# Value products over two 64-key halves side by side, summed by VectorE, in a talking-heads attention with a linear expert

## The chip, the cores and the metric

The kernel runs on one core of one Trainium2 chip. The time is the device time of one execution in microseconds (us). Three runs of the kernel before gave 1441.68, 1441.87 and 1443.87 us; the median, 1441.87 us, is what the change is measured against.

## The reference

Eight batches of 12 heads, 448 positions, 64 channels per head. The scores are mixed across heads before the softmax and the weights are mixed across heads after it; then come the value products, and the joined heads go through a bilinear layer and two linear ones:

```python
scores = scale * np.matmul(q, k.transpose(0, 1, 3, 2))
scores = np.einsum('bhij,hg->bgij', scores, w_pre)
attn = np.exp(scores - np.max(scores, axis=-1, keepdims=True))
attn = attn / (np.sum(attn, axis=-1, keepdims=True) + 1e-09)
attn = np.einsum('bhij,hg->bgij', attn, w_post)
attn_out = np.matmul(attn, v)
x = attn_out.transpose(0, 2, 1, 3).reshape(B * S, H * D)
out = ((x @ w1) * (x @ w2)) @ w3 @ w_out
```

The change touches only `attn_out = attn @ v`, for batches 2 to 7.

## The kernel before

**Steps.** The queries of a batch are cut into 45 tiles of 10 (the last has 8). One step `n` of the main loop in `run` belongs to one such tile; two tiles are worked on together, so even and odd steps differ. A step holds these pieces, and every engine executes its instructions in the order in which `run` writes them (nothing is reordered by a scheduler):

- the expert's matmuls, handed out by `advance` in a number per step that a table `shares` sets (tiles `eg` and `eo` for the first two batches, then `e`, `e1o`, `e2o`, `e3o` by pairs of batches; lines 522, 553, 702);
- in some odd steps, the value products `av` (line 301, PSUM tile `psa`);
- in odd steps, `post` (line 260, tile `pso`): the head mix after the softmax, 56 small matmul instructions that also turn the weights so that keys lie on partitions; then `mix` (line 220, tile `psm`): the head mix before the softmax; then `qk` (line 174, tile `psq`): scores of a coming batch, which go to HBM and are read back by head.

ScalarE copies `pso` into `mt` (line 274) and `psq` into `st` (lines 179 and 180), takes the exponentials (line 235), and VectorE takes the row extremes from `psm` (line 227).

**The value products.** `mt` holds the mixed weights of 150 queries (15 tiles; the last stretch of a batch has 148), with 128 keys on the partitions and four key blocks `j`. Keys are 448 = 3 x 128 + 64. In the fourth block each partition half holds the same 64 keys: `post` writes the last key block of row half `s` to partition half `s`, and zeros, set once before the loop, stand in the other half. So in block 3 the first 64 partitions hold only the queries 0 to 4 of each ten, and the last 64 partitions only the queries 5 to 9; `layouts` doubles the last 64 rows of `v` to match. `av(b, a, g)` handles one pair of heads `g` in stretch `a` (0, 1, 2) of batch `b`: for each key block and each of the two heads one fp32 matmul with 128 contraction rows and 64 output columns, which the profile shows as two MATMUL records. Three pairs share a PSUM bank and are emitted in one step; the next three come two steps later. So a batch has 6 such groups of 3 calls, 4 of them 150 queries wide and 2 of them 148 wide.

**PSUM banks.** `psa` and the first `psq` of a step's `qk` use bank 0; the second half of `qk` uses bank 1; `psm` uses 2 and 3, `pso` 4 and 5, the expert 6 and 7. For batches from the third on (`b >= ONE`, `ONE = 2`), ScalarE copies a finished `psa` bank to an SBUF tile `xd` (line 308), and the next step's start issues its store to `x_d` in HBM on the SyncE queue. In the first two batches ScalarE writes `xh` from the bank and VectorE then reads the bank again for `xl` (lines 322 and 323).

`ends` holds the closing work (PSUM reads) of groups with their bank numbers; `do_ends` emits it. `bank(i)` emits pending closing work first if bank `i` is among it.

Of the kernel before, what the change touches and what calls it, by code (L numbers as in the profile page):

```python
# [10 lines left out]
ALU = mybir.AluOpType  # L11
# [4 lines left out]
B, H, S, D = 8, 12, 448, 64  # L16
DM, FF = 768, 1024
HP = H // 2
IB = 10
GI = H * IB  # L20
NB = -(-S // IB)
QT, NJ = 128, 4
GB = 15
NG = NB // GB
KF, K1 = FF // 128, DM // 128
IH = IB // 2
HK = H * IH
PP = 64
# [9 lines left out]
ONE = 2  # L38
# [12 lines left out]
class Kernel:  # L51
# [237 lines left out]
    def cols(self, a):  # L289
        return slice(a * GB * IB, min((a + 1) * GB * IB, S))  # L290

    def av(self, b, a, g):
        nc, cols = self.nc, self.cols(a)
        W = cols.stop - cols.start
        if g % 3 == 0:
            self.psa = self.bank(0, f"psa{b}_{a}_{g}")[:, :3 * GB * IB].rearrange("p (g i) -> p g i", g=3)
        v, mt = self.vs[b, g], self.mt[b, a]
        for j in range(NJ):
            for s in range(2):
                rows = slice(s * D, (s + 1) * D)  # L300
                nc.tensor.matmul(self.psa[rows, g % 3, :W], v[:, j, rows], mt[:, j, 2 * g + s, :W],  # L301
                                 start=(j == 0), stop=(j == NJ - 1))
        if g % 3 == 2 and b >= ONE:
            q, dst = self.psa[:, :, :W], self.x_d[b][g // 3][:, :, cols]
            x = self.xq.tile([128, 3, GB * IB], F32, tag="x", name=f"xd{b}_{a}_{g}")[:, :, :W]

            def leave():
                nc.scalar.copy(x, q)
                self.later.append(store)

            def store():
                nc.sync.dma_start(dst, x)
                self.x_made[b] += 1

            self.ends.append((0, leave))
        elif g % 3 == 2:
            if b not in self.xs:
                pool = self.xp[b % 2]
                self.xs[b] = [pool.tile([128, K1, S], F32R, tag=f"x{t}", name=f"x{t}{b}") for t in "hl"]
            h, l = (x[:, g - 2:g + 1, cols] for x in self.xs[b])  # L320
            q = self.psa[:, :, :W]
            self.ends.append((0, lambda: nc.scalar.copy(h, q)))
            self.soon.append((0, lambda: nc.vector.tensor_tensor(l, q, h.bitcast(F32), op=ALU.subtract)))
        if a == NG - 1:
            self.later.append(self.load_v)
# [726 lines left out]
```

## Time and profile before

| what | value |
|---|---|
| median of 3 runs | 1441.87 us (1441.68 to 1443.87) |
| the profiled execution's own time | 1437.83 us |
| its span, first to last instruction | 1436.1 us |
| mean granted TensorE clock | 0.986 |
| MATMUL records of the value products | 2304, of them 1728 in batches 2 to 7 |
| groups of three calls in batches 2 to 7 | 36 (24 of 150 queries, 12 of 148) |
| their first and last start | 398.2 and 1262.5 us |
| ScalarE copies `xd` | 36, median 535 ns |

TensorE's busy time counts records whose ends are modelled; the starts of matmuls are what tells their pace. "PE" are matmuls, "PEld" weight loads, which overlap matmuls. In the timeline, a row gives start, length, engine, line, operation, tiles, shapes and how many records were merged; in the chain of waits a row gives start, length, and what was on the path that ended last.

### The profile page before, as it was taken

To read this page: it belongs to the slowest core of one execution; us is meant where nothing else is said; L and a number is where in the kernel's file an instruction comes from. 1 tells how busy PE (TensorE), PEld (TensorE's weight loads), DVE (VectorE), ACT (ScalarE), POOL (GpSimd) and SP (SyncE) were. 2 spreads that over 40 slices of the span, in tenths; PEclk is the share of its full clock that TensorE was granted. 3 is DMA by queue.
4 is the path that set the end of the run, shared out by engine and by line. 5 is a ranking of instruction groups with operands and counts; after the bars stand their busy time and mean duration, and the time that the engine had idled before them with its cause. 6 is when DMAs were issued, how large, how long until landed. Compare 5 with 4: busy or idle time off the path is not lost.

```text
span 1436.1 us, 45775 instructions
## 1 busy us (share of the span) xinstructions
PE 1382.4 (96%) x18684; PEld 1055.2 (73%) x18684; DVE 741.1 (52%) x1497; ACT 832.4 (58%) x1952; POOL 620.3 (43%) x754
## 2 busy tenths in 40 slices
PE   5889999999999999999999999999999999999998
PEld 2457786776677667776777777777777777899988
DVE  6867566767544544432444436334444446345563
ACT  4867666777766666665656556556555445422231
POOL 2433233434433544532345336334335446446693
PEclk7989999999999999999999999999999999999999
DMA  8998789999999999999989979799879757698775
GB/s 294 366 326 279 236 270 322 320 312 317 324 286 348 355 356 330 362 346 349 287 275 290 320 259 280 249 323 354 288 229 281 241 177 223 195 337 270 231 232 171
DMA packets 203761, 416.87 MB, mean 290 GB/s; under 512 B 20528, under 2 KB 120112, under 8 KB 203472
## 3 DMA queue, kind: packets, MB, share of 16 engines
q1 hardware_dynamic: 203552, 413.94, 87.6%
q8 instruction: 149, 2.44, 0.7%
q14 instruction: 60, 0.49, 0.1%
HBM read 279.77 MB, written 134.09 MB: 288 GB/s over the span
## 4 chain that ended last, share of the span: by engine, by line
PE 82%; DMA 8%; DVE 4%; ACT 2%; issue 1%; POOL 1%; SPq 0%; DVEq 0%; POOLq 0%; ACTq 0%
PE e L702 21%; PE psa L301 11%; PE pso L260 10%; PE psm L220 9%; PE psq L174 7%; PE eg L522 5%; PE psf L360 4%; PE eo L553 4%; PE e2o L702 4%; PE e1o L702 4%; PE e3o L702 4%; DMA wu<-w_d 3%; DMA r<-raw_d 2%; DMA raw_d<-st 2%; ACT e L235 1%
## 5 line engine op out<-in xcount | busy, mean ns | idle before, releaser
L247 POOL TENSOR_SCALAR w<-wpo,ri 128x60 f32<-128x60 f32 x360 | 180.7, 518 | 485.1 <-DVE ri L245 465.3
L227 DVE TENSOR_REDUCE mn<-psm 128x1 f32<-128x448 f32 x360 | 207.7, 618 | 321.6 <-PE psm L220 321.3
L274 ACT COPY mt<-pso 128x480 f32<-128x480 f32 x352 | 197.9, 621 | 185.8 <-PE pso L260 185.6
L702 PE MATMUL e<-eh,wu 128*128 128x448 f32 x1008 | 296.8, 371 | 6.4 <-DVE c L656 3.2
L235 ACT ACTIVATE e<-psm,mn 128x448 f32<-128x448 f32 x360 | 226.8, 643 | 7.9 <-DVE mn L227 7.9
L702 PEld LDWEIGHTS e<-eh,wu 128*128 128x128 f32 x1008 | 187.5, 188 | 52.2 <-issue 26.8
L260 PEld LDWEIGHTS pso<-w,e 60*64 60x64 f32 x10080 | 175.2, 135 | 51.0 <-issue 42.5
L220 PE MATMUL psm<-r,wsc 60*64 60x448 f32 (+1 forms) x1440 | 191.2, 550 | 19.1 <-DVE cx L124 8.3
L260 PE MATMUL pso<-w,e 60*64 60x60 f32 x10080 | 199.1, 224 | 0.4 <-ACT mt L274 0.3
L702 PE MATMUL e<-el,wu 128*128 128x448 f32 x504 | 186.9, 371 | 0.0
L301 PE MATMUL psa<-mt,v 128*64 128x150 f32 (+1 forms) x2304 | 156.9, 292 | 4.1 <-ACT st L179 4.1
L301 PEld LDWEIGHTS psa<-mt,v 128*64 128x64 f32 x2304 | 143.6, 137 | 20.1 <-ACT st L179 6.7
L174 PE MATMUL psq<-kq 64*64 64x448 f32 x1176 | 154.6, 542 | 2.4 <-ACT st L179 2.4
L656 DVE TENSOR_TENSOR c<-c,e 128x448 f32<-128x448 f32 x168 | 101.7, 618 | 87.7 <-PE e L702 82.9
L179 ACT COPY st<-psq 128x448 f32<-128x448 f32 x162 | 86.4, 533 | 73.7 <-ACT mt L274 34.1
L522 PE MATMUL eg<-xh,wu 128*128 128x448 f32 x384 | 119.2, 381 | 6.3 <-DMA wu<-w_d 6.3
L641 POOL TENSOR_TENSOR el<-x,eh 128x448 fp32r<-128x448 f32 x90 | 103.7, 1170 | 32.8 <-ACT eh L640 29.9
L702 PEld LDWEIGHTS e<-el,wu 128*128 128x128 f32 x504 | 94.6, 188 | 22.5 <-issue 14.1
L174 PEld LDWEIGHTS psq<-kq 64*64 64x64 f32 x1176 | 60.8, 135 | 56.4 <-issue 28.8
L522 PEld LDWEIGHTS eg<-xh,wu 128*128 128x128 f32 x384 | 71.9, 190 | 38.7 <-issue 24.0
L244 DVE TENSOR_SCALAR sa<-sm 128x2 f32<-128x2 f32 x180 | 34.9, 194 | 113.6 <-ACT e L235 113.1
L180 ACT COPY st<-psq 128x448 f32<-128x448 f32 x162 | 87.6, 541 | 0.0
(99 smaller groups left out, 2010.1 us busy)
## 6 DMA issues: line engine op xcount, KB each, us to landing
r<-raw_d SPq DMA_DIRECT2D x344, 210.0 KB, 5.1
raw_d<-st SPq DMA_DIRECT2D x138, 448.0 KB, 6.1
wu<-w_d SPq DMA_DIRECT2D x104, 384.0 KB, 6.7
wu<-s_d SPq DMA_DIRECT2D x96, 384.0 KB, 4.8
wu<-w_d SPq DMA_DIRECT2D x51, 512.0 KB, 5.5
kq<-kq SPq DMA_DIRECT2D x42, 448.0 KB, 7.0
wu<-s_d SPq DMA_DIRECT2D x36, 512.0 KB, 4.9
x<-x_d SPq DMA_DIRECT2D x72, 224.0 KB, 5.7
```

The source lines that it names most:

```text
L174: nc.tensor.matmul(ps[s][z * PP:(z + 1) * PP], t[rows, q:q + PP], t[rows, k:k + S], start=True, stop=True)
L220: nc.tensor.matmul(ps[s][c * PP:(c + 1) * PP, :S], self.wsc[k], r[k, c], start=True, stop=True)
L227: self.nc.vector.tensor_reduce(mn[:, s:s + 1], self.psm[m][s][:, :S], axis=AX.X, op=ALU.min)
L235: nc.scalar.activation(e, p[:, :S], AF.Exp, bias=mn[:, s:s + 1], scale=-1.0, accum_out=sm[:, s:s + 1])
L247: nc.gpsimd.tensor_scalar_mul(w2[:, s], self.wpo, ri[:, s:s + 1])
L260: nc.tensor.matmul(self.pso[c][z * PP:(z + 1) * PP, at:at + HK], e[k, j * PP:(j + 1) * PP], w2s[k, s], start=True, stop=True)
L274: self.nc.scalar.copy(dst.rearrange("p j g (s i) -> p j s g i", s=2), src)
L301: nc.tensor.matmul(self.psa[rows, g % 3, :W], v[:, j, rows], mt[:, j, 2 * g + s, :W], start=(j == 0), stop=(j == NJ - 1))
L522: nc.tensor.matmul(p, u[:, k % (K1 // 2), x], xs[y][:, k], start=(k == 0 and t == 0), stop=(k == K1 - 1 and t == 2))
L641: nc.gpsimd.tensor_tensor(lo, x, hi.bitcast(F32), op=ALU.subtract)
L656: nc.vector.tensor_tensor(a[out], a[to[0]], p, op=ALU.add)
L702: nc.tensor.matmul(p, w[:, k, x], ops[m, k][y], start=(k == 0 and t == 0), stop=(k == nk - 1 and t == 2))
```

## The change

For batches 2 to 7 `av` opens two banks, 0 and 1. Key blocks 0 to 2 are cut into partition halves: the products of keys on partitions 0 to 63 go to bank 0, those on 64 to 127 to bank 1. Block 3 is taken for each half with the columns in which that half is not zero: 5 queries of each ten, through a three-dimensional view (`halves`), and where the stretch is 148 wide a second piece of 5 or 3 columns for the incomplete tile. After ScalarE's copy of bank 0, VectorE adds bank 1 to it. Batches 0 and 1 keep their products.

```diff
+    def halves(self, w, z):
+
+        n = w // IB
+        yield lambda t: t[:, :n * IB].rearrange("p (u s i) -> p u s i", s=2, i=IH)[:, :, z]
+        if w % IB:
+            yield lambda t: t[:, n * IB + z * IH:min(n * IB + (z + 1) * IH, w)]
+
     def av(self, b, a, g):
...
         if g % 3 == 0:
-            self.psa = self.bank(0, f"psa{b}_{a}_{g}")[:, :3 * GB * IB].rearrange("p (g i) -> p g i", g=3)
+            self.psa = [self.bank(z, f"psa{b}_{a}_{g}_{z}")[:, :3 * GB * IB].rearrange("p (g i) -> p g i", g=3)
+                        for z in range(1 + (b >= ONE))]
         v, mt = self.vs[b, g], self.mt[b, a]
-        for j in range(NJ):
+        for j in range(NJ - (b >= ONE)):
             for s in range(2):
                 rows = slice(s * D, (s + 1) * D)
-                nc.tensor.matmul(self.psa[rows, g % 3, :W], v[:, j, rows], mt[:, j, 2 * g + s, :W],
-                                 start=(j == 0), stop=(j == NJ - 1))
+                for z, psa in enumerate(self.psa):
+                    keys = slice(z * PP, (z + 1) * PP) if b >= ONE else slice(0, 128)
+                    nc.tensor.matmul(psa[rows, g % 3, :W], v[keys, j, rows], mt[keys, j, 2 * g + s, :W],
+                                     start=(j == 0), stop=(j == NJ - 1), skip_group_check=b >= ONE)
+        if b >= ONE:
+            for s in range(2):
+                rows = slice(s * D, (s + 1) * D)
+                for z, psa in enumerate(self.psa):
+                    keys = slice(z * PP, (z + 1) * PP)
+                    for part in self.halves(W, z):
+                        nc.tensor.matmul(part(psa[rows, g % 3]), v[keys, NJ - 1, rows], part(mt[keys, NJ - 1, 2 * g + s]),
+                                         start=False, stop=True, skip_group_check=True)
         if g % 3 == 2 and b >= ONE:
-            q, dst = self.psa[:, :, :W], self.x_d[b][g // 3][:, :, cols]
+            (q, r), dst = (t[:, :, :W] for t in self.psa), self.x_d[b][g // 3][:, :, cols]
...
                 nc.scalar.copy(x, q)
+                nc.vector.tensor_tensor(x, x, r, op=ALU.add)
                 self.later.append(store)
...
-            self.ends.append((0, leave))
+            self.ends += [(0, leave), (1, lambda: None)]
```

On TensorE, the end of the first group of batch 2. Before (`eo` is the expert's matmul ahead, `psa_0_0` the group's bank, x8 are the eight matmuls of one head pair):

```order
L553 MATMUL eo_0_5896<-eh_4_4931,wu_5796 128x448
L301 MATMUL psa_0_0_5984<-mt_0_5258,v_0_5280 64x150 x8
L301 MATMUL psa_0_0_5984<-mt_0_5258,v_1_5282 64x150 x8
L301 MATMUL psa_0_0_5984<-mt_0_5258,v_2_5284 64x150 x8
L260 MATMUL pso_141<-w_5885,e_0_5864 64x60
L260 MATMUL pso_142<-w_5885,e_0_5864 64x60
```

Now, the last rows of the third pair (`psa_0_0_0` is in bank 0, `psa_0_0_1` in bank 1):

```order
L311 MATMUL psa_0_0_0_5984<-mt_0_5258,v_2_5284 64x150
L311 MATMUL psa_0_0_1_5985<-mt_0_5258,v_2_5284 64x150
L319 MATMUL psa_0_0_0_5984<-mt_0_5258,v_2_5284 64x15x5
L319 MATMUL psa_0_0_1_5985<-mt_0_5258,v_2_5284 64x15x5
L319 MATMUL psa_0_0_0_5984<-mt_0_5258,v_2_5284 64x15x5
L319 MATMUL psa_0_0_1_5985<-mt_0_5258,v_2_5284 64x15x5
L260 MATMUL pso_141<-w_5885,e_0_5864 64x60
L260 MATMUL pso_142<-w_5885,e_0_5864 64x60
```

A pair is 8 matmuls before and 16 now: 12 of full width and 4 of 75 columns. In a group of 148 queries it is 20; there the fourth block reads as follows, with two matmuls in a row on the same half:

```order
L311 MATMUL psa_2_0_1_7541<-mt_2_6774,v_0_5280 64x148
L319 MATMUL psa_2_0_0_7540<-mt_2_6774,v_0_5280 64x14x5
L319 MATMUL psa_2_0_0_7540<-mt_2_6774,v_0_5280 64x5
L319 MATMUL psa_2_0_1_7541<-mt_2_6774,v_0_5280 64x14x5
L319 MATMUL psa_2_0_1_7541<-mt_2_6774,v_0_5280 64x3
```

On VectorE at the same group, before (`sa`, `ri` belong to the softmax's sums, `y` to sums of expert weights, `mn` are the row extremes that wait for `psm`):

```order
L244 TENSOR_SCALAR sa_5976<-sm_5961 128x2
L245 RECIPROCAL ri_5977<-sa_5976 128x2
L463 TENSOR_TENSOR y_0_5954<-wu_5796 128x512
L227 TENSOR_REDUCE mn_6061<-psm_0_6039 128x1
L227 TENSOR_REDUCE mn_6061<-psm_1_6040 128x1
```

Now:

```order
L244 TENSOR_SCALAR sa_5976<-sm_5961 128x2
L245 RECIPROCAL ri_5977<-sa_5976 128x2
L482 TENSOR_TENSOR y_0_5954<-wu_5796 128x512
L327 TENSOR_TENSOR xd_0_2_6034<-xd_0_2_6034,psa_0_0_1_5985 128x450
L227 TENSOR_REDUCE mn_6087<-psm_0_6065 128x1
L227 TENSOR_REDUCE mn_6087<-psm_1_6066 128x1
```

The add stands between the softmax's small operations and the next row extremes, 36 times in all. ScalarE's and SyncE's rows keep their order, and no transfer is added. Of the 36 groups, 34 are followed by `pso` (the last two by `e`), and 28 of these by `psm` and then `psq`.

More of the change, by code (lines that the diff above doesn't have):

```diff
@@ L320, in av @@
             h, l = (x[:, g - 2:g + 1, cols] for x in self.xs[b])
-            q = self.psa[:, :, :W]
+            q = self.psa[0][:, :, :W]
             self.ends.append((0, lambda: nc.scalar.copy(h, q)))
```

## The prediction

> **What bounds the kernel now.** First the page's busy times and its chain of waits, by engine and by line:
>
> ```profile
> PE 1382.4 (96%) x18684; PEld 1055.2 (73%) x18684; DVE 741.1 (52%) x1497; ACT 832.4 (58%) x1952; POOL 620.3 (43%) x754
> PE 82%; DMA 8%; DVE 4%; ACT 2%; issue 1%; POOL 1%; SPq 0%; DVEq 0%; POOLq 0%; ACTq 0%
> PE e L702 21%; PE psa L301 11%; PE pso L260 10%; PE psm L220 9%; PE psq L174 7%; PE eg L522 5%; PE psf L360 4%; PE eo L553 4%; PE e2o L702 4%; PE e1o L702 4%; PE e3o L702 4%; DMA wu<-w_d 3%; DMA r<-raw_d 2%; DMA raw_d<-st 2%; ACT e L235 1%
> ```
>
> TensorE is the path, and the value products are 11% of it. Then the windows (columns: PE, PEld, DVE, ACT, POOL busy with counts, granted clock, DMA share, GB/s), since the changed groups run from 398 to 1262 us, and TensorE's waits between 380 and 700 us:
>
> ```profile
> 400.00:500.00 100.00, 97.68 (x1558) 72.55 (x1554) 47.29 (x96) 62.83 (x148) 41.06 (x46) 1.00 0.98 333
> 600.00:700.00 100.00, 97.55 (x1479) 72.79 (x1478) 31.63 (x77) 62.16 (x149) 29.52 (x45) 1.00 1.01 344
> 800.00:900.00 100.00, 99.68 (x1474) 75.97 (x1473) 48.00 (x101) 59.98 (x140) 47.31 (x58) 1.00 0.88 283
> PE eg L522 <- DMA wu<-w_d: 6.3, 5, 2.8
> ```
>
> Up to about 700 us the DMA engines are as full as TensorE; after that TensorE alone is. A third of the groups (12: the 8 wide and 4 narrow of batches 2 and 3) lies in the first stretch. There TensorE waited 6.3 us, five times, for expert weights.
>
> The chain in order of time around the first changed group, and a 148-wide one:
>
> ```profile
> 395.79 2.43 PE eo L553 x11
> 398.22 3.21 PE psa L301 x48
> 401.43 1.01 PE pso L260 x47
> 402.44 0.76 PE psm L220 x8
> ...
> 494.18 3.17 PE psa L301 x48
> ```
>
> So a group's 3.21 us (3.17 at 148) are on the path whole. How they are made up, the timeline of TensorE over short stretches shows:
>
> ```profile
> 398.15 0.35 PE L301 MATMUL psa<-mt,v 128*64 128x150 f32 x2
> 398.15 0.48 PE L301 MATMUL psa<-mt,v 128*64 128x150 f32 x4
> 400.75 0.68 PE L301 MATMUL psa<-mt,v 128*64 128x150 f32 x8
> 401.13 0.30 PE L301 MATMUL psa<-mt,v 128*64 128x150 f32 x2
> 401.36 0.28 PE L260 MATMUL pso<-w,e 60*64 60x60 f32 x4
> 401.36 0.34 PE L260 MATMUL pso<-w,e 60*64 60x60 f32 x8
> 401.36 0.57 PE L260 MATMUL pso<-w,e 60*64 60x60 f32 x24
> 402.22 0.54 PE L220 MATMUL psm<-r,wsc 60*64 60x448 f32 x1
> 402.23 0.22 PE L260 MATMUL pso<-w,e 60*64 60x60 f32 x1
> 402.98 0.98 PE L174 MATMUL psq<-kq 64*64 64x448 f32 x8
> ```
>
> Records start in rounds. Value products go two abreast (the two heads' 64 columns): the last 8 records take 0.68 us, the last 2 0.30, so three rounds are 0.38 and one is 0.127 us. A group is 24 rounds, 3.05 us. The 64 x 64 products go four abreast: `pso`'s records 9 to 24 add 0.57 - 0.34 = 0.23 us in four rounds, 0.058 each at 60 columns; `psm`'s 8 records, two rounds at 448 columns, take from 402.22 to 402.98, 0.38 each. And a change of shape costs: `psa`'s last round begins at 401.13, so the next could at 401.26, but `pso` starts at 401.36, 0.10 late; and `pso`'s second round begins 0.10 after the first (0.34 less a record's 0.22 and the stagger of 0.02) in place of 0.058. Together 0.145 us. Between `pso`, `psm` and `psq`, all 64 x 64, there is no such gap.
>
> **The change, part by part.**
>
> *Rounds of 64 x 64.* A half-key matmul has `pso`'s form and order (row half 0, row half 1, next column half), so I cost it four abreast. No row has 150 columns in that form; the straight line through 60 columns (0.058) and 448 (0.38) has 0.83 ns a column and gives 0.133 us at 150, 0.131 at 148, 0.0705 at 75 and 0.066 at 70. The other end is the two-abreast price, 0.127 and its half, 0.064. I take the line: its rows have the same shape.
>
> - 150 wide: 36 full logical matmuls are 18 rounds, 12 of 75 columns are 6. 18 x 0.133 + 6 x 0.0705 = 2.82 us against 3.05: 0.23 saved. At the other end 0.37.
> - 148 wide: before, 3.05 - (3.21 - 3.17) = 3.01. Now 18 x 0.131 + 6 x 0.066, and 6 rounds more of 5 or 3 columns. A round that short is between the line's 0.012 and the 0.058 of 60 columns; I take 0.058, because weights are loaded for it all the same. Sum 3.10: 0.09 lost (at the other end 0.18 saved).
>
> 24 x 0.23 - 12 x 0.09 = **4.4 us**.
>
> *Shape changes.* The expert ahead of the group is 128 x 128, so entering costs the same: the second round starts 0.48 - 0.30 = 0.18 after the first against 0.127 now, and would again. Leaving for `pso` is now without a change of shape: 34 groups x 0.145 = **4.9 us**. The two last groups go to the expert and gain nothing here.
>
> *Strided columns.* Block 3 reads and writes 5 of each ten floats. No matmul of the trace does. The nearest rows are ScalarE's copies, one into runs of five, one plain:
>
> ```profile
> L274 ACT COPY mt<-pso 128x480 f32<-128x480 f32 x352 | 197.9, 621 | 185.8 <-PE pso L260 185.6
> L179 ACT COPY st<-psq 128x448 f32<-128x448 f32 x162 | 86.4, 533 | 73.7 <-ACT mt L274 34.1
> ```
>
> 621 ns / 480 is 1.29 ns a column, 533 / 448 is 1.19: 9% dearer. The streams concerned are 24 x 6 x 75 and 12 x 6 x 70 columns at 0.83 ns, 13.1 us. Bounds: nothing, and all of 13.1 (every skipped float paid for). I take the 9%, **1.1 us** lost. [...]
>
> *Evacuation.* The ACT copy stays; 36 adds of the size of `xl` come to VectorE. Every copy found ScalarE waiting for it (116.0 us in 36 waits), and VectorE is idle at that place. Rows: who waited for `psa`; VectorE after a group in the pair stage; then the same pattern as the new one in batch 0, where ScalarE's copy and VectorE's read of one bank stand between `psa` and `psq`:
>
> ```profile
>   ACT xd L308: 116.0, 36
> ...
> 852.75 0.62 DVE L227 TENSOR_REDUCE mn<-psm 128x1 f32<-128x448 f32 x1 [3.68 <-PE psm L220]
> ...
> 99.52 1.08 PE L260 MATMUL pso<-w,e 60*64 60x60 f32 x55
> 99.63 0.53 ACT L322 CAST xh<-psa 128x450 fp32r<-128x450 f32 x1 [0.96 <-PE psa L301]
> 100.20 0.63 DVE L323 TENSOR_TENSOR xl<-psa,xh 128x450 fp32r<-128x450 f32 x1 [1.13 <-ACT xh L322]
> 100.88 0.45 PEld L174 LDWEIGHTS psq<-kq 64*64 64x64 f32 x7 [0.30 <-DVE xl L323]
> 101.14 0.59 PE L174 MATMUL psq<-kq 64*64 64x448 f32 x3
> ```
>
> `psq` in bank 1 now waits for the add, as there for `xl`. There the weight load waited 0.30 us, yet `psq` began 1.62 us after `pso`, exactly as at 401.36 to 402.98, where nothing held it. Queued behind `psq` on TensorE is the expert, so a wait would be paid in full. After the change `psa`'s end lies about 0.10 later relative to `pso` (last round one 0.07 ahead of `pso` with some 0.24 to run, against 0.23 ahead with 0.30), and `pso`'s faster first round brings `psq` 0.045 forward. Release at 1.36 + 0.10 = 1.46 us after `pso`'s start, matmul due at 1.575: it fits with 0.1 us to spare. I take 0.02 us for each of 28 groups, **0.6 us**; without the cover it is the add's 0.63 each. The add is done before `mn` is due, and the store goes out in the next step, later than the add. Opening bank 1 also makes a group wait for the copy at line 180; over 2.4 us of expert work lie between, so nothing.
>
> *Transfers.* None is added. In the full stretch the 12 groups save 8 x 0.375 + 4 x 0.055 = 3.2 us. The chain runs through every one of these groups, which says it is kept; the DMA share of 1 says that weights come no sooner. I take half, **1.6 us** given back.
>
> Sum: 4.4 + 4.9 - 1.1 - 0.6 - 1.6 = 6.0 us. The profiled execution took 1437.83 us and would take 1431.8. That execution is 4 us under the median of the three runs shown, so I carry the difference over: 1441.87 - 6.0 = **1435.9 us**.
>
> **The rivals.**
>
> 1. *Strided halves pay for every float they skip* (slower side). Place: the fourth block. 4.4 + 4.9 - 13.1 - 0.6 = 4.4 us lost, with no transfer loss since nothing is gained: 1446.3. It decides from a slowdown of 1.7 on (9.3 / 13.1). [...] Against: 9% on ScalarE, and 0.83 ns a column is slow enough that a stride may hide.
> 2. *VectorE becomes the gate of `psq`.* If something of VectorE's stands before the add, 28 x 0.63 = 17.6 us more: 1453. Against: the idle 3.68 us above.
> 3. *Halves in a row on one tile block the others*, in the 148-wide block, where four records in a row go to one quarter of the array. Started strictly in order, each quarter begins only when the one before has started its fourth record, 0.066 + 0.066 + 0.058 = 0.19 us later, and the next pair after 0.76 us in place of 0.25: 36 calls x 0.51 = 18 us, 1454. Against: the rows at 402.22 and 402.23, where `psm` starts before `pso`'s last, which stands ahead of it in the program. [...]
> 4. *The halves don't run side by side at all.* 18 rounds more a group, 36 x 18 x 0.133 = 86 us: 1528. Against: `pso` and `psm` do.
> 5. *Small parts cancel* (a stride factor about 1.5, some wait of `psq`): within 0.2%, 1441.
>
> **How the numbers follow.** Forecast 0.70; rivals 1 to 5: 0.11, 0.05, 0.03, 0.02, 0.09. 0.2% (2.9 us) is about what a measurement of this kernel can tell from no change. The forecast's own range is 1428 (two-abreast prices: 24 x 0.37 + 12 x 0.18 + 4.9 = 15.9, less 1.6 and some stride) to 1439. The whole range reaches over rivals 1 and 5: 1428 to 1446.5. Faster 0.71, same 0.10, slower 0.19.
>
> **What would show it.** In the profile after: 64 x 64 `psa` records four abreast, with rounds of 0.133 and 0.07; a group of 2.8 us on the chain (3.1 at 148), followed by `pso` at 0.87 in place of 1.01; `psq` still beginning 1.6 us after `pso`; the add ending before `mn` starts; TensorE's waits for weights before 700 us grown by some 2 us. A round of 0.13 at 75 columns proves rival 1; `psq` ended by VectorE with matmul idle, rival 2; quarters of the array starting one after another in the narrow block, rival 3. A median above 1439 makes the forecast wrong.

## The result and the profile after

The changed kernel takes 1454.77 us (median of 5 runs, 1452.27 to 1459.09) against 1441.87 us (1440.63 to 1443.87) in the same session: ratio 1.0089, 95% interval 1.0066 to 1.0112. It is slower by 12.9 us; the prediction said 6 us faster, with 1446.5 as its upper end. The profiled execution of after took 1459.09 us, with a span of 1457.3 us.

The page of after, first its busy times, then a DMA queue, then the chain of waits by engine and by line:

```profile
PE 1384.3 (95%) x20700; PEld 1057.8 (73%) x20700; DVE 764.2 (52%) x1533; ACT 834.3 (57%) x1952; POOL 621.2 (43%) x754
...
q8 instruction: 164, 2.69, 0.8%
...
PE 79%; DMA 10%; DVE 4%; issue 3%; ACT 3%; SPq 1%; POOL 1%; DVEq 0%; POOLq 0%; ACTq 0%
PE e L721 20%; PE pso L260 10%; PE psm L220 9%; PE psa L311 9%; PE psq L174 7%; PE eg L541 5%; PE psf L379 4%; PE eo L572 4%; PE e2o L721 4%; PE e3o L721 4%; DMA wu<-w_d 4%; PE e1o L721 3%; DMA r<-raw_d 2%; DMA raw_d<-st 1%; PE psa L319 1%
```

The value products fell from 11% of the chain to 10% (9% and 1%). "issue", time in which the engine waited for nothing that the profile shows, rose from 1% to 3%. TensorE has 2016 matmul records more and as many weight loads, and the queue of kind "instruction" moved 164 packets. The page of before has for that queue:

```profile
q8 instruction: 149, 2.44, 0.7%
```

Where the change is made, it does what was forecast. The timeline of after around the first changed group (the counterpart of the rows at 398.15 to 402.98 of before):

```profile
396.32 0.99 PE L311 MATMUL psa<-mt,v 64*64 64x150 f32 x24
397.13 0.32 PE L319 MATMUL psa<-mt,v 64*64 64x75 f32 x8
397.28 0.94 PE L311 MATMUL psa<-mt,v 64*64 64x150 f32 x24
398.05 0.32 PE L319 MATMUL psa<-mt,v 64*64 64x75 f32 x8
398.19 0.94 PE L311 MATMUL psa<-mt,v 64*64 64x150 f32 x24
398.96 0.31 PE L319 MATMUL psa<-mt,v 64*64 64x75 f32 x8
399.10 1.03 PE L260 MATMUL pso<-w,e 60*64 60x60 f32 x55
...
399.39 0.54 ACT L326 COPY xd<-psa 128x450 f32<-128x450 f32 x1 [3.14 <-PE psa L319]
399.95 0.62 DVE L327 TENSOR_TENSOR xd<-xd,psa 128x450 f32<-128x450 f32 x1 [2.65 <-ACT xd L326]
400.63 0.24 PEld L174 LDWEIGHTS psq<-kq 64*64 64x64 f32 x7 [0.20 <-DVE xd L327]
400.67 0.98 PE L174 MATMUL psq<-kq 64*64 64x448 f32 x8
```

From the first value product to `pso` are 2.78 us (396.32 to 399.10) where 3.21 were; a 148-wide group takes 3.03 (3.17 before). Over all 36 groups the stretch from `psa`'s start to `pso`'s, leaving out stops, sums to 103.5 us against 115.1: **11.6 us gained**. `psq` starts 1.57 us after `pso` (1.62 before).

The loss stands elsewhere. TensorE's waits in after (what waited, for what: us in all, times, the longest):

```profile
PE psm L220 <- DMA r<-raw_d: 11.1, 3, 7.4
PE pso L260 <- issue: 10.4, 5, 2.8
...
PE psq L174 <- issue: 2.8, 2, 1.8
...
PE psm L220 <- issue: 1.8, 1, 1.8
```

The same view of before has no row with "issue". One of the stops, in the timeline and in the chain of waits of after:

```profile
602.57 0.74 PE L260 MATMUL pso<-w,e 60*64 60x60 f32 x32
606.08 0.50 PE L260 MATMUL pso<-w,e 60*64 60x60 f32 x19 [2.77 <-issue]
```
```profile
602.74 0.57 PE pso L260 x32
603.31 2.77 issue
606.08 0.50 PE pso L260 x16
```

In the middle of `pso`'s 56 matmuls, which all read the same two kinds of tile (`w` and `e`), TensorE stands still for 2.77 us; no semaphore, engine or transfer of data is named. Nine such stops, from one matmul's start to the next 1.35 to 2.99 us, together 19.9 us, lie in this profile. What they have in common is shown when TensorE's records (weight loads, matmuls and some 700 others) are numbered from the start of the span. A count of mine over the trace, not a view of the profile:

```
record      stop from..to      block used up in   next block usable after
14785      503.26.. 504.61        2.79 us              4.14 us
16065      544.20.. 546.50        3.68                 5.98
18113      603.10.. 606.08        3.31                 6.30
19393      643.13.. 646.03        2.83                 5.73
24769      809.47.. 811.96        2.83                 5.32
28353      917.14.. 919.50        3.14                 5.50
30401      978.35.. 980.15        2.90                 4.70
31937     1028.61..1030.19        3.76                 5.34
35777     1143.73..1145.80        4.13                 6.20
```

Every number is 193 more than a multiple of 256. A "block" here is the 256 records up to that number. A packet of the instruction queue has 16384 bytes (2.69 MB in 164), 64 for each of 256; and TensorE's records, 42118 in after and 38106 in before, divided by 256 are 164.5 and 148.9, the packets of the two pages. In each stop a packet started 2.3 to 2.7 us ahead of TensorE's going on. So my theory after the result: **TensorE's instructions arrive in blocks of 256; where a block is used up faster than the next one comes, TensorE stands.** A wide group was 96 records and is 192, a narrow one was 96 and is 240, `pso`'s 112 follow in 0.87 us; in the profile of before the fastest block lasted 5.2 us. A fast block is not enough for a stop: by the same count four more blocks of after were used up in 3.1 to 3.7 us (they begin at 758, 866, 1130 and 1188 us) and ended in no stop, or in one of 0.29 us. Their next packets had started between 2.9 us ahead of the block's begin and 0.9 us behind it; in the nine stops the packet started 1.6 to 3.8 us behind it.

### The profile page after: what moved, and what is told of

The parts are those of the page before. It is cut to its first block, busy times and chain, and to the rows that moved or that the text cites. A ratio compares the mean times of both kernels' runs of the same rounds, so it can differ in the third digit from the quotient of the medians.

```text
span 1457.3 us, 49847 instructions
## 1 busy us (share of the span) xinstructions
PE 1384.3 (95%) x20700; PEld 1057.8 (73%) x20700; DVE 764.2 (52%) x1533; ACT 834.3 (57%) x1952; POOL 621.2 (43%) x754
## 3 DMA queue, kind: packets, MB, share of 16 engines
q8 instruction: 164, 2.69, 0.8%
## 4 chain that ended last, share of the span: by engine, by line
PE 79%; DMA 10%; DVE 4%; issue 3%; ACT 3%; SPq 1%; POOL 1%; DVEq 0%; POOLq 0%; ACTq 0%
PE e L721 20%; PE pso L260 10%; PE psm L220 9%; PE psa L311 9%; PE psq L174 7%; PE eg L541 5%; PE psf L379 4%; PE eo L572 4%; PE e2o L721 4%; PE e3o L721 4%; DMA wu<-w_d 4%; PE e1o L721 3%; DMA r<-raw_d 2%; DMA raw_d<-st 1%; PE psa L319 1%
## 5 line engine op out<-in xcount | busy, mean ns | idle before, releaser
L260 PEld LDWEIGHTS pso<-w,e 60*64 60x64 f32 x10080 | 178.8, 136 | 55.7 <-issue 49.2
L220 PE MATMUL psm<-r,wsc 60*64 60x448 f32 (+1 forms) x1440 | 197.3, 556 | 20.3 <-DMA r<-raw_d 11.1
L260 PE MATMUL pso<-w,e 60*64 60x60 f32 x10080 | 201.8, 224 | 11.1 <-issue 10.4
L174 PE MATMUL psq<-kq 64*64 64x448 f32 x1176 | 161.7, 548 | 5.7 <-ACT st L179 2.9
L311 PE MATMUL psa<-mt,v 64*64 64x150 f32 (+3 forms) x3168 | 143.5, 291 | 2.2 <-ACT st L179 2.2
L311 PEld LDWEIGHTS psa<-mt,v 64*64 64x64 f32 (+1 forms) x3168 | 116.1, 134 | 18.3 <-issue 6.4
L174 PEld LDWEIGHTS psq<-kq 64*64 64x64 f32 x1176 | 64.2, 136 | 56.1 <-issue 25.8
```

The costliest lines, as they stand in the source:

```text
L174: nc.tensor.matmul(ps[s][z * PP:(z + 1) * PP], t[rows, q:q + PP], t[rows, k:k + S], start=True, stop=True)
L220: nc.tensor.matmul(ps[s][c * PP:(c + 1) * PP, :S], self.wsc[k], r[k, c], start=True, stop=True)
L260: nc.tensor.matmul(self.pso[c][z * PP:(z + 1) * PP, at:at + HK], e[k, j * PP:(j + 1) * PP], w2s[k, s], start=True, stop=True)
L311: nc.tensor.matmul(psa[rows, g % 3, :W], v[keys, j, rows], mt[keys, j, 2 * g + s, :W], start=(j == 0), stop=(j == NJ - 1), skip_group_chec ...
```

## The experiments

The rivals to instruction supply were the things that the change does beside adding records: half-key products in two banks, the add, the strided columns, transfers that come earlier. Nine kernels ran, and the kernel before twice more, in four sessions; each is compared with the kernel before in its own session (medians 1444.04, 1442.94, 1445.36 and, for the last, one run of 1444.83 us).

**Only the records: e1.** The kernel before, with each value product of batches 2 to 7 as two of half the columns. One bank, no add, no half keys, no stride over queries; 192 records a group.

```diff
-        for j in range(NJ):
-            for s in range(2):
-                rows = slice(s * D, (s + 1) * D)
-                nc.tensor.matmul(self.psa[rows, g % 3, :W], v[:, j, rows], mt[:, j, 2 * g + s, :W],
-                                 start=(j == 0), stop=(j == NJ - 1))
+        half = W // 2
+        for part in ((slice(0, half), slice(half, W)) if b >= ONE else (slice(0, W),)):
+            for j in range(NJ):
+                for s in range(2):
+                    rows = slice(s * D, (s + 1) * D)
+                    nc.tensor.matmul(self.psa[rows, g % 3, part], v[:, j, rows], mt[:, j, 2 * g + s, part],
+                                     start=(j == 0), stop=(j == NJ - 1), skip_group_check=b >= ONE)
```

> The kernel before, with each value product of batches 2 to 7 issued as two products of half the columns (75 and 75, or 74 and 74): the same 128 x 64 form, one bank, no add, the same sums; only the number of TensorE records in a group doubles, from 96 to 192. Theory (instruction supply): TensorE's records arrive in blocks of 256; in the profile of the change TensorE stands still 1.4 to 3.0 us, nine times, each time at the same place within a block, when the block before was used up in 2.8 to 4.1 us, and goes on about 5.5 us after that block was begun. Laid over the trace of before with 192 records a group and 4.5 to 5.5 us a block, that gives 9 to 22 us of such stops: slower than before by 9 to 22 us. Rival (the second bank, the add, the waits they bring): none of it is in this kernel, so within 2 us of before.

1451.11 us (8 runs), ratio 1.0043 (1.0026 to 1.006): some 6 us slower. The timeline and the waits of e1:

```profile
397.69 3.35 PE L303 MATMUL psa<-mt,v 128*64 128x75 f32 x96
400.97 1.08 PE L260 MATMUL pso<-w,e 60*64 60x60 f32 x55
```
```profile
PE pso L260 <- issue: 2.5, 3, 1.7
```

A group takes 3.28 us in place of 3.21: 36 x 0.066 = 2.4 us. Stops at 193 modulo 256 came, without any half-key product: 1.93 us at 652, 0.84 at 712 and 0.38 at 1137. They are fewer than in after because a group that is 0.5 us longer gives blocks of 3.4 us and more in place of 2.8. The expectation's lower end, 9 us, was too high: I had taken every block to need 4.5 to 5.5 us.

**Half keys with few records: e2.** Blocks 0 to 2 stay whole; only the fourth is taken in halves of 75 columns, for the three pairs together at the group's end, in the 24 wide groups: 120 records. The second half's columns go to bank 1, and VectorE adds those alone.

```diff
-        for j in range(NJ):
+        for j in range(NJ - split):
...
+        if split and g % 3 == 2:
+            for f in range(g - 2, g + 1):
+                for s in range(2):
+                    rows = slice(s * D, (s + 1) * D)
+                    for z, ps in enumerate((self.psa, self.psr)):
+                        keys = slice(z * PP, (z + 1) * PP)
+                        nc.tensor.matmul(half(ps[rows, f % 3], z), self.vs[b, f][keys, NJ - 1, rows],
+                                         half(mt[keys, NJ - 1, 2 * f + s], z), ...)
```

> Key blocks 0 to 2 stay whole (128 keys, one bank); only block 3 is taken in two halves with half the columns, for the three pairs of a group one after another at its end, in groups of 150 queries; groups of 148 stay as before. The second half's columns go to bank 1 and VectorE adds only those. A wide group has 120 records in place of 96 (the change has 192). Theory (instruction supply): with the same count over the trace of before, blocks of 256 last 5 us or more, so no stop; the group falls by 24 x 0.127 - 18 x 0.127 - 6 x 0.07 = 0.34 us, 24 groups 8 us, less up to 2 us to transfers: 6 to 8 us faster than before. Rival (bank 1 and the add cost the time): they are here too in 24 of 36 groups, so slower than before by two thirds of the change's loss, some 8 us, or no faster than before.

1437.23 us (12 runs), ratio 0.9963 (0.9945 to 0.9981): faster by 5 us, where 6 to 8 were expected. Its timeline:

```profile
397.78 2.52 PE L304 MATMUL psa<-mt,v 128*64 128x150 f32 x36
...
400.71 0.98 PE L260 MATMUL pso<-w,e 60*64 60x60 f32 x54
```

2.93 us a group (397.78 to 400.71); no matmul of e2 waits for "issue", and its shortest blocks last 4.5 us. So two banks, an add and strided columns cost nothing that shows, and the shape change moves into the group.

**No add: e3.** The change without VectorE's add (the sums over the keys on partitions 64 to 127 are left out of the output).

```diff
                 nc.scalar.copy(x, q)
-                nc.vector.tensor_tensor(x, x, r, op=ALU.add)
```

> The change without VectorE's add of bank 1, so the sums over keys on partitions 64 to 127 are left out of the output for batches 2 to 7; every matmul stays. Theory (instruction supply): the records on TensorE are the change's, so the time is the change's within 3 us, 9 to 15 us above before. Rival (the add or the wait for bank 1 costs the time): without them the forecast's 6 us gain appears, about 1436.

1452.54 us (4 runs), ratio 1.0064 (1.004 to 1.0089). The waits of e3:

```profile
PE pso L260 <- issue: 9.1, 6, 2.5
...
PE psm L220 <- issue: 3.9, 2, 2.2
...
PE psq L174 <- issue: 1.5, 1, 1.5
```

Nine stops of 17.4 us in all, at the very nine record numbers of after. The add is not the cause.

**The same program, 200 records later: e4.** 50 matmuls that mean nothing at the front shift the block borders through the program.

```diff
+        for _ in range(SHIFT):
+            nc.tensor.matmul(dps[:PP, :8], dm[:, :PP], dm[:, PP:], start=True, stop=True)
```

> The change with 50 tiny matmuls of zeros (200 records) put ahead of all other TensorE work, where TensorE waits for the first loads anyway. Their results are used by nobody. Theory (instruction supply): the limits of the blocks of 256 records move by 200, and so does the set of dense places that fall into one block. Laid over the trace of the change with the stops taken out, at 5.0 to 5.5 us a block, the stops add up to 35 to 37 us in place of 22 to 31: slower than the change by 6 to 13 us, and standing still at another count within the block. Rival (bank, add, transfers): the time of the change within 2 us.

1462.85 us (4 runs), ratio 1.014 (1.0118 to 1.0161), 8 us above the change. Of that 6.7 us lie at the front, where the first `pso` starts at 41.07 us in place of 34.35; so the time itself tells little. The stops tell more: 14 over 0.5 us, 23.4 us in all, again at 193 modulo 256, and so at other places of the program (the first two in after are at 503 and 544 us, here at 409 and 520). A cause in the data or in a certain step would have stayed where it was. Two parts of the expectation missed: the count within the block stayed at 193, because the 200 new records are counted too, and the stops add up to 23.4 us, not to 35 to 37.

**Supply by itself: e7.** The kernel before, with two bursts of 384 matmuls of 64 x 64 by 8 columns, in `pso`'s order, six blocks each.

```diff
+    def burst(self):
+        dps = [self.bank(r, f"dps{r}") for r in range(2)]
+        for i in range(96):
+            for c in range(2):
+                for r in range(2):
+                    keys = slice(PP * r, PP * r + PP)
+                    self.nc.tensor.matmul(dps[r][PP * c:PP * c + PP, :8], self.dm[keys, :PP], self.dm[keys, PP:], ...)
```

> The kernel before with two bursts of work that means nothing: 384 matmuls of 64 x 64 by 8 columns each time (768 matmul and 768 weight-load records, six blocks of 256), in the order of pso's, once in the stretch where the DMA engines are full and once in the pair stage where they are not. By the pace of pso (112 records in 0.87 us) each burst would take 12 us without a stop. Theory (instruction supply): what has been brought ahead, one to two blocks, goes at that pace; after that a block takes what its supply takes, 2.2 to 5 us, with stops at one count modulo 256: a burst of 16 to 27 us, longer in the stretch where the DMA engines are full. Rival (supply keeps up with 2 us a block; the stops of the change come from what value products do): 12 us each, no stop.

One run, 1485.16 us. The timeline of e7 at the first burst, then windows (as in the prediction: PE, PEld, DVE, ACT, POOL busy, granted clock, DMA share, GB/s), then the queues between 570 and 582 us:

```profile
558.57 3.67 PE L299 MATMUL dps<-dm 64*64 64x8 f32 x237
566.22 3.60 PE L299 MATMUL dps<-dm 64*64 64x8 f32 x128 [3.98 <-issue]
569.98 3.60 PE L299 MATMUL dps<-dm 64*64 64x8 f32 x128 [0.16 <-issue]
574.01 3.59 PE L299 MATMUL dps<-dm 64*64 64x8 f32 x128 [0.44 <-issue]
577.76 3.60 PE L299 MATMUL dps<-dm 64*64 64x8 f32 x128 [0.15 <-issue]
```
```profile
562.20:566.10 3.90, 0.04 (x2) 0.00 (x0) 0.00 (x0) 0.00 (x0) 0.00 (x0) 0.50 0.92 287
570.00:574.00 4.00, 3.58 (x128) 3.48 (x128) 0.00 (x0) 0.00 (x0) 0.00 (x0) 0.50 0.01 4
```
```profile
q8 instruction: 3, 0.05, 1.5%
```

128 matmuls with their weight loads are one block, and the burst goes on in pieces of 128. The rest of the running block and one more had been brought (237 matmuls at once). That whole block was used up in 1.89 us, and the next was usable 6.07 us after it was begun, 4.18 us of it a stop, at a DMA share of 0.92. Later, with the DMA engines idle (0.01), the blocks followed each other every 3.76 to 4.03 us, and in the second burst every 3.48 to 4.03 (5.94 for its first short block, with a stop of 4.09 us at a DMA share of 1.05). A block began 2.3 to 2.6 us after its packet had started. With idle DMA engines the packet started 1.1 to 1.7 us after the block ahead was begun, under full ones 3.4 to 3.5. So the price of a block is its fetch, some 3.5 to 4 us when nothing else is moved and about 6 when the engines are full, and one block is all that lies ahead. The later pieces ran at a granted clock of 0.50, where 128 matmuls take 3.35 us; that is why the stops between them are short. The first burst took 24 us (558.6 to 582.5) and the second 23.3, within the expected 16 to 27, where `pso`'s pace gives 12. These totals decide less than the two stops of over 4 us, since the half clock stretches the later blocks; and the second burst was not the shorter one by much, because the DMA engines were full at its start too.

**The change, spread out: e5 and e8.** Both were to issue expert matmuls between the value products and `pso`, so that the dense 256 records last longer.

```diff
e5:
-            advance(now - now // 2)
+            between = now - now // 2 if avs.get(n) and avs[n][0][0] >= ONE else 0
+            advance(now - now // 2 - between)
...
+            self.do_ends()
+            advance(between)
e8:
+            kept, keep = keep, 0
+            if avs.get(n + 1) and avs[n + 1][0][0] >= ONE:
+                keep = now - now // 2
...
-            advance(now - now // 2)
+            advance(now - now // 2 - keep)
...
+            advance(kept)
             if odd and 1 <= m <= SETS:
                 self.post(m - 1)
```

> The change, with the same records on every engine; only in the steps with value products of batches 2 to 7 the second half of the step's expert matmuls is issued between the value products and pso instead of ahead of the value products. So the dense stretch (144 or 192 weight loads and matmuls of the value products, then pso's 112) is broken by expert matmuls, which take some 0.2 us each. Locally it costs: the step from the value products to pso, 0.145 us, which the change had saved, comes back as a step to the expert and one from it, about 0.3 us for each of 34 groups, 10 to 14 us. Theory (TensorE's instructions come in blocks of 256 and a block that is used up in under about 4.5 us leaves TensorE standing): the dense blocks now last 5 us or more, the stops at count 193 modulo 256 shrink from 19.9 us to under 4, and the two effects leave the time at 1443 to 1452 us, 3 to 12 us under the change. Rival (the loss hangs on the values' banks, on the add or on transfers, not on the density): the stops stay, and the shape changes come on top, 1462 to 1470 us.

e5 missed its aim: steps with value products hand out no expert work, so its instructions are those of the change in the same order. It is a second measurement of the change: 1455.87 us (5 runs), ratio 1.008 (1.0051 to 1.0108). Its profile has stops at the same nine record numbers, with other lengths (0.83 to 2.88 us, 15.5 in all). The places are the program's. The lengths follow the packets: a block could be used 2.4 to 2.6 us after its packet had started, and the packets started 1.1 to 3.5 us after the block ahead was begun.

> The change with the same matmuls, banks and adds; ahead of every group of value products of batches 2 to 7 the second half of the preceding step's expert matmuls is held back and issued between the value products and pso (in the run e5 nothing was held back, because steps with value products hand out no expert work of their own). Locally this costs the 0.145 us step from psa to pso again and one more step, 0.25 to 0.3 us in each of 34 groups: 8.5 to 10 us, of which the profile will show a psa-to-pso time of about 2.8 us plus the expert work. Theory (a block of 256 TensorE records that is used up in under 4 us leaves it standing): the dense blocks now last 4.5 us and more, the stops at count 193 modulo 256 fall from 16 to 20 us to under 5; time 1443 to 1453 us. Rival (stops come from the half-key products themselves, the two banks or the add): the stops stay, 1460 to 1468 us.

1458.11 us (5 runs), ratio 1.009 (1.0061 to 1.0119). The timeline at the first group of e8 and its waits:

```profile
400.61 0.32 PE L319 MATMUL psa<-mt,v 64*64 64x75 f32 x8
400.85 0.47 PE L572 MATMUL eo<-el,wu 128*128 128x448 f32 x1
...
402.27 1.08 PE L260 MATMUL pso<-w,e 60*64 60x60 f32 x55
```
```profile
PE psm L220 <- DMA r<-raw_d: 14.3, 4, 7.5
...
PE pso L260 <- issue: 2.4, 4, 1.4
...
PE psm L220 <- issue: 0.4, 1, 0.4
...
PE psq L174 <- issue: 0.3, 1, 0.3
```

At the nine numbers the blocks now last 4.3 to 5 us and more; seven of the nine stops are left over 0.3 us, the longest 1.61, together 5.7 in place of 19.9 and 15.5. So half of the expectation holds: lengthening the same blocks takes most of the stops away, with banks, add and stride unchanged. The other half, the time, does not: nothing was gained. Most steps with a group became 0.3 to 0.4 us longer, a few up to 0.8, for the two more shape changes, some 12 us in all where I had 8.5 to 10, and the waits for expert weights and for scores are 5 to 6 us longer than in the two profiles of the change. These eat the 10 to 14 us of stops.

**Fewer records: e9 and e6.** Both fill the narrow groups up to 150 columns with zeros, so that every group has one form: e9 the change (192 records in all groups), e6 e2's form (120 in all groups).

```diff
+                if a == NG - 1 and b >= ONE:
+                    nc.gpsimd.memset(self.mt[b, a][:, :, :, S - a * GB * IB:], 0.0)
...
+        if b >= ONE:
+            W = GB * IB
...
-                nc.sync.dma_start(dst, x)
+                nc.sync.dma_start(dst, x[:, :, :n_out])
```

> The change, but the narrow groups are filled up from 148 to 150 columns with columns of zeros, so that the fourth block needs no second piece: 192 records in every group in place of 240 in the 12 narrow ones. In the profile after, 5 of the 9 long stops follow one of the 12 narrow groups and 4 one of the 24 wide ones. Theory (supply): a narrow group takes 2.78 us in place of 3.03, 3 us in all, and the stops shrink by 3 to 8 us because fewer blocks are used up fast; they do not go. 1444 to 1450 us. Rival (only the matmuls of 5 and 3 columns cause the stops): no stop is left, 1432 to 1436 us.

e9: 1445.33 us (10 runs), ratio 1.0004 (0.998 to 1.0028), level with the kernel before. The waits of e9:

```profile
PE pso L260 <- issue: 4.7, 3, 2.8
PE psm L220 <- issue: 3.8, 2, 2.4
```

Six stops of 0.5 us and more at 193 modulo 256 are left, 10.4 us in all, the longest 3.01, though no matmul of 5 or 3 columns is. So these are not the cause; fewer records brought fewer stops, as the supply theory had it.

> Key blocks 0 to 2 stay whole; only the fourth is taken in halves of 75 columns, at the end of a group, as in e2, now in all 36 groups: the narrow ones are filled up to 150 columns with two columns of zeros. 120 records a group in place of 96. Local theory and instruction supply agree here: a group of 2.93 us as in e2's wide groups, so 12 more groups gain about 0.24 us each, 2.9 us beyond e2, 8 us under the kernel before (1433 to 1437 us); no stop over 0.3 us at count 193 modulo 256. Rival (any half-key product brings the stops): no better than the kernel before.

e6: 1432.68 us (6 runs), ratio 0.9936 (0.9913 to 0.996), 9 us faster than before. A narrow group in its timeline:

```profile
495.58 2.52 PE L308 MATMUL psa<-mt,v 128*64 128x150 f32 x36
...
498.51 1.04 PE L260 MATMUL pso<-w,e 60*64 60x60 f32 x55
```

2.93 us (3.17 before), and no wait for "issue". It is the best of the kernels run, ahead of before and of the change.

**The kernel before, twice more: before_again.** No edit.

> The kernel before, unchanged, for a second profile. Open is whether the 3.5 us that TensorE waits for scores read back (psm, from raw_d) in the profile of before is typical: every kernel with shorter groups shows 11 to 14 us there. If shorter groups give their gain back in the stretch where the DMA engines are full, the wait is 3 to 6 us here again; if the one profile of before was a lucky one, 9 to 13 us, with a span some 6 us longer.

> The same again: 3 to 6 us of waits for scores read back if the give-back is real, 9 to 13 us if the profile of before was a lucky one.

Spans of 1443.9 and 1440.3 us, and for scores 12.6 and 3.1 us: neither answer as it was put. The difference is one long wait at the program's start. The timelines of before and of the first of the two, and then of after, have it at the same place:

```profile
18.16 1.85 PE L220 MATMUL psm<-r,wsc 60*64 60x448 f32 x5 [8.26 <-DVE cx L124]
```
```profile
17.72 1.95 PE L220 MATMUL psm<-r,wsc 60*64 60x448 f32 x5 [7.43 <-DMA r<-raw_d]
```
```profile
18.64 2.47 PE L220 MATMUL psm<-r,wsc 60*64 60x448 f32 x7 [7.41 <-DMA r<-raw_d]
```

The profile puts it down now to VectorE, now to the transfer. So the 7.6 us by which this wait seems longer in after than in before are no loss of the change. The three spans (1436.1, 1443.9, 1440.3) say further that the profile on which the prediction was made is a short one. And before is not quite free of stops: the first of these two profiles has one of 0.85 us at 193 modulo 256, at 1019 us, where a packet came late for a block of 8.7 us.

## Why the prediction was wrong

**The step that failed** is the costing of records by rounds: "A half-key matmul has `pso`'s form and order (row half 0, row half 1, next column half), so I cost it four abreast", 192 and 240 records a group at 0.133 and 0.07 us a round. The rounds came as priced, but the step took for granted that the next instruction is there: no term of the sum stands for bringing the instructions. `pso`, the row that gave the price, has only 112 records in a row; 192 or 240 ahead of these make a block of 256 last 2.8 to 4.1 us. Shown: the same nine numbers in three runs of the same records (after, e5, e3), other places with shifted records (e4), stops from records alone (e1), shorter stops with longer blocks (e8), fewer with fewer (e9, e6), and the fetch's own price (e7). The missing term is 19.9 us in the profile of after (15.5 in e5's, 17.4 in e3's), and it is larger than the 11.6 us that the groups gained.

The sum for that profile, against the mean of the three spans of before (1440.1): 11.6 us gained in the groups, 19.9 lost in stops. Beyond that, by the granted clock in the trace, after has 20.5 us at half clock between 380 and 1400 us, and the three profiles of before have 3.4, 10.2 and 6.8; 13.7 us more at half speed cost up to 6.9. Together up to 15.2, of the 17.2 us measured; the rest is less than the three spans of before differ by. The same sum gives 7.4 of 9.8 us for e5's profile and 5.8 of 6.8 for e3's. That the half clock costs all of this is an estimate; no run takes it away alone, and not all of it belongs to the stops: 10.2 of the 20.5 us come right behind stops (at 607, 921 and 1146 us), the rest behind waits of some 3 us for scores and for expert weights. e8's profile has no half clock in that stretch, and its time is no better.

**Point by point.**

- *Rounds*: right. Six full rounds and two of 75 columns take 0.77 and 0.14 us inside a group, 0.128 and 0.07 each (0.133 and 0.0705 forecast). A wide group went to 2.78 us (forecast 2.82), a narrow one to 3.03 (3.10).
- *Shape change*: right. `pso` follows the value products at once, and e8, which puts it back with one more, pays about 0.35 us a group.
- *Strided columns*: 1.1 us was forecast, nothing is seen: the 75-column rounds, 0.07 us, have about half the length of those of 150, 0.128. Block 3 was read and written in runs of five floats.
- *Evacuation*: right. The add ran at 399.95, behind the copy; the weight load waited 0.20 us, the matmul not at all. Over all groups five weight loads waited for the add, 0.9 us together, and no matmul of `psq` did, so the 0.6 us forecast were not paid.
- *Transfers*: 1.6 us was forecast as given back. The sign named for it, waits for weights grown by some 2 us before 700 us, is not there: from 380 to 700 us TensorE waited 6.5 us for `eg`'s weights where it was 6.3. The waits for scores in that stretch are 3.0 us where they were 1.8, too little to tell from the spread of before's own waits.
- *Rivals*: 1 (stride), 2 (VectorE gates `psq`) and 4 (not side by side) are excluded by the rows of the first group, 3 (halves block one another) by the narrow groups' 3.03 us, where it asked for 0.51 more for each of three calls. 5 (parts cancel) is out by its time. The slower result came by a mechanism that was on no list, though the page of before has the queue that brings the instructions.

## What to carry to other kernels

Count an engine's records, not only their time: where a change multiplies small TensorE instructions, ask how long a block of them (256 records here) lasts at the densest place, and what a fetch costs there (in this kernel 3.5 to 4 us with idle DMA engines, about 6 with full ones). A short block does not always cost a stop: four of after, of 3.1 to 3.7 us, ended in none or in one of 0.29 us, where the next packet had started between 2.9 us ahead of the block's begin and 0.9 us behind it. A gain per group that comes from more and shorter instructions can be lost between the groups; the same idea applied only where it saves most (here the fourth key block: 120 records in place of 192 or 240) gained 9 us in the end, where the whole change won 11.6 us in its groups and lost more between them. When stops have no releaser, number the records and look at the stops' numbers modulo a block.

## What was unexpected of the hardware

- TensorE's supply: blocks of 256 records, one ahead; a period of 3.5 to 4 us at a DMA share near 0 (0.01 to 0.04 in the windows of e7), of 4.1 to 6.3 us in the stops of after. No run shows more ahead than the rest of one block and the next: in e7 the first burst ran 237 matmuls with their weight loads at once, the second 235.
- Behind three of the nine stops of after the granted clock was 0.50 for 3.4 us (at 607, 921 and 1146 us). Windows of after behind the stops at 603 and 917 us:

```profile
606.00:609.50 3.50, 3.42 (x40) 1.85 (x39) 1.16 (x2) 1.12 (x2) 0.00 (x0) 0.60 0.42 144
919.50:923.00 3.50, 3.50 (x17) 1.81 (x18) 2.50 (x5) 1.32 (x3) 0.00 (x0) 0.67 0.28 69
```

  TensorE worked nearly all of these windows, yet the granted clock was 0.60 and 0.67. What half the clock does is seen in e7: right behind the first burst, still at 0.50, the row of `pso`'s 56 matmuls is 1.81 us long, where it is 1.03 in the rows of after shown above. In the trace the clock falls to 0.50 for stretches of 3.4 us or small multiples of it (3.4, 6.8 and 10.2 us in after, 23.9 us in each burst of e7). Not every stop is followed by one: behind that of 2.90 us at 643 the clock stayed at 1.00. Which stops are is left open.
- In e7's bursts the clock stayed at 0.50 although TensorE was busy for 3.58 of 4.00 us. These matmuls are small (64 x 64 by 8 columns) and multiply zeros; whether one of the two or something else held the clock down, no run here tells.
